# Four rows' statistics moved from VectorE to ScalarE in an SSM kernel's first batch, and a reordered parameter chain behind it

## The chip, the cores and the metric

The kernel runs on one core of one Trainium2 chip. The metric is the device time of one execution in microseconds (us). Before the change it is 687.45 us, the median of three runs (686.68 to 687.59).

## What is computed

The reference is a block with two halves. First a layer normalisation of `u` (2048 tokens x 448 channels), modulated by vectors made from `c`, goes through a long convolution whose kernel is a sum of 256 damped oscillations per channel (S4D). Then a token-mixing MLP follows.

```python
dt = jnp.exp(log_dt)
A = -jnp.exp(log_A_real) + 1j * A_imag
C = (C_real + 1j * C_imag) * dt[:, None]
P = jnp.exp((A * dt[:, None])[:, :, None] * pos[None, None, :])
K = 2.0 * jnp.einsum("dn,dnl->dl", C, P).real
Kf = jnp.fft.rfft(K, L2); Uf = jnp.fft.rfft(u_t, L2)
y = jnp.fft.irfft(Uf * Kf[None, :, :], L2)[:, :, :L]
...
h = _layernorm(x, axis=-1) * (1 + ca) + sa
x = x + ga * _A_ref(h, ...)
h = _layernorm(x, axis=-1) * (1 + cb) + sb
x = x + gb * _B_ref(h, ...)          # W2 gelu(W1 LayerNorm(h))
```

What matters here: the layer normalisation needs mean and variance of all 2048 tokens, and the kernel `K` needs, for each channel and oscillation, a log magnitude (the "exponents") and an angle (the "phases").

## The kernel before

**Stages.** The 448 channels are worked in 28 groups of 16, two steps per group, so 56 steps, in sets of eight (`BATCH`). The whole first part (to about 380 us) makes the convolution kernel step by step and, beside it, normalises and transforms the input; then comes the MLP, which is matmul after matmul. Instructions of TensorE (PE), ScalarE (ACT), VectorE (DVE) and GpSimd (POOL) stand in an order written out by hand; each engine runs its own list in that order and waits where an input isn't there yet.

**A set.** At the first step of each set `window(s)` (L1024) runs first: ScalarE takes logarithms and exponentials there, eight pairs of exponentials into `mag` (L650), with one table of functions. Then follow the eight steps with the table of sines. So ScalarE's table is changed twice a set.

**A step s** is: TensorE's `st_phase(s+1)` (L639, angles into the PSUM tiles `xe` and `xg`, two buffers of each); ScalarE's `st_abs(s)` (L676, L677) and four sines (L686 to L689, two of them in place in `xe` and `xg`); GpSimd's two products `G` (L691, L692) and a magnitude `m` for a later step (L666, L668); VectorE's four products `E` (L693, L694, L698, L699, each 128 x 512), which read `xe` and `xg`; and `st_kgen` (L722), which multiplies `E` and `G` on TensorE. ScalarE copies the result out after every second step (L736), and VectorE adds to it (L741).

**Beside the steps of the first set** (`s` from 0 to 7), in `between()` behind a step's four `E`, VectorE takes the statistics of the input's 16 rows of tiles: `u_stats(r)`, one `bn_stats` and one `bn_aggr` (L537, L538), six rows before step 0 and ten rows by the table `late_rows`, one or two behind each of steps 0 to 5. Row r's mean and variance go to `mv[:, r]`. ScalarE's `logs` in the window of step 8 takes their square roots by logarithm and exponential (L471, L472, tile `rs`), VectorE makes the factor and the shift (`u_scale`, L542 to L546, tile `nm`), GpSimd or ScalarE normalises the rows (L553, L551), and TensorE transforms them (`u_rows`, tile `pu`, L563). VectorE multiplies the result by the modulation into `yt` (L566).

**The parameter chain.** The first 128 channels' parameters are made at the start; those of the second, third and fourth 128 (`chain(q)`, q = 1, 2, 3) are made a few small VectorE instructions at a time: `more(n)` runs the next n pieces of the generator, up to a point ("logs") where it waits for ScalarE's logarithms in the next window. The table `WPACE` says how many pieces each of a window's eight stages e runs, `pace` how many each step runs. Behind the window's logarithms the chain made first the exponents' part (L426, L428 and splits into two halves, L393, L395), then the phases' part (L433 to L443), then the start angle (L447 to L459).

**Deferred work.** `act` and `dve` are lists of deferred instructions that `flush` puts out. What is put on `act` in `between()` stands on ScalarE's list behind that step's sines, and ahead of the next step's.

Of the kernel before, what the change touches and what calls it, by code (L numbers as in the profile page):

```python
# [11 lines left out]
F32 = mybir.dt.float32  # L12
F32R = mybir.dt.float32r
BF16 = mybir.dt.bfloat16
AF = mybir.ActivationFunctionType
ALU = mybir.AluOpType
# [5 lines left out]
L, D, N, F = 2048, 448, 256, 1792  # L22
P = 128
# [10 lines left out]
MAGIC = 1.5 * 2.0**23  # L34
# [187 lines left out]
def tile_adaln_s4d_mixer(ctx, tc, i, out):  # L222
# [21 lines left out]
    with ExitStack() as es:  # L244
        V, S, G, T = nc.vector, nc.scalar, nc.gpsimd, nc.tensor
        tt, ts, stt = V.tensor_tensor, V.tensor_scalar, V.scalar_tensor_tensor
# [19 lines left out]
        xp = spec.enter_context(tc.tile_pool(name="xp", bufs=1))  # L266
# [33 lines left out]
        xt = xp.tile([P, 16, D], F32, name="xt")  # L300
# [37 lines left out]
        for q in range(4):  # L338
            r = slice(32 * q, 32 * q + 1)
# [31 lines left out]
        dt4 = qp.tile([P, 4], F32, name="dt4")  # L371
# [4 lines left out]
        dve, act, late_act = [], [], []  # L376
# [5 lines left out]
        def chain(q):  # L382


            w = N if q < 3 else P
            cr, ci, a, aim = (raws[q][nm][:, 0:w] for nm in ("A_C_real", "A_C_imag", "A_log_A_real", "A_A_imag"))
            xa, ya, s, t, u, ph, p64 = (
                qp.tile([P, N], F32, tag=nm, name=nm)[:, 0:w] for nm in ("xa", "ya", "s", "t", "u", "ph", "p64")
            )

            def split(src, to):
                hl = qp.tile([P, 2, N], F32R, tag="hl", name="hl", bufs=3)[:, :, 0:w]
                V.tensor_copy(hl[:, 0], src)  # L393
                yield
                tt(hl[:, 1], src, hl[:, 0].bitcast(F32), ALU.subtract)  # L395
                for k, v in to:
                    if q < 3:
                        nc.sync.dma_start(pars[q][v, k], hl.bitcast(F32))
                        continue
                    for h in range(2):  # L400
                        r = slice(64 * h, 64 * h + 64)
                        nc.sync.dma_start(pars[q][v, k, 0:64, :, P * h : P * h + P], hl[r].bitcast(F32))
                yield


            S.activation(xa, cr, AF.Abs, scale=0.5)
            S.activation(ya, ci, AF.Abs, scale=0.5)
            stt(s, xa, 2.0**-120, ya, ALU.max, ALU.add)
            yield
            tt(ya, ya, xa, ALU.subtract)  # L410
            yield
            V.reciprocal(xa, s)
            yield
            tt(ya, ya, xa, ALU.mult)
            yield

            ts(t, s, 2.0**-40, 2.0**80, ALU.is_lt, ALU.mult)
            yield
            stt(s, t, 1.0, s, ALU.max, ALU.mult)
            yield  # L420
            tmp[q] = a, s, u, xa, ya
            while q in tmp:
                yield "logs"
            ya = u
            yield from split(a, [(0, 1), (1, 1)])
            stt(s, t, -80 * math.log(2.0) / 2.0**80, s, ALU.mult, ALU.add)  # L426
            yield
            tt(s, ya, s, ALU.add)  # L428
            yield
            yield from split(s, [(2, 1)])  # L430
            yield "exponents"

            ts(ph, aim, dt4[:, q : q + 1], None, ALU.mult)  # L433
            yield
            ts(u, ph, MAGIC, MAGIC, ALU.add, ALU.subtract)
            yield
            tt(ph, ph, u, ALU.subtract)
            yield
            yield from split(ph, [(0, 0)])

            ts(u, ph, MAGIC / 128, MAGIC / 128, ALU.add, ALU.subtract)
            yield
            tt(p64, ph, u, ALU.subtract)  # L443
            yield
            yield from split(p64, [(1, 0)])

            ts(u, cr, 0.0, 0.5, ALU.is_ge, ALU.subtract)  # L447
            yield
            tt(xa, xa, u, ALU.mult)
            yield  # L450
            ts(u, ci, 0.0, 0.5, ALU.is_ge, ALU.subtract)
            yield
            stt(xa, xa, 0.5, u, ALU.add, ALU.mult)
            yield
            stt(xa, ph, 63.0, xa, ALU.mult, ALU.add)
            yield
            ts(u, xa, MAGIC, MAGIC, ALU.add, ALU.subtract)
            yield
            tt(xa, xa, u, ALU.subtract)  # L459
            yield  # L460
            yield from split(xa, [(2, 0)])
# [69 lines left out]
        mv = xp.tile([P, 16, 2], F32, name="mv")  # L531
        rs = xp.tile([P, 16], F32, name="rs")
        nm = xp.tile([P, 16], F32, name="nm")

        def u_stats(r):
            st = xp.tile([P, 6], F32, tag="st", name="st", bufs=2)
            V.bn_stats(st, xt[:, r])  # L537
            V.bn_aggr(mv[:, r], st)  # L538

        def u_scale():  # L540

            tt(nm, rs, rs, ALU.mult)  # L542
            stt(nm, mv[:, :, 1], EPS, nm, ALU.add, ALU.mult)
            ts(nm, nm, -0.5, 1.5, ALU.mult, ALU.add)
            tt(rs, rs, nm, ALU.mult)
            stt(nm, mv[:, :, 0], -1.0, rs, ALU.mult, ALU.mult)  # L546
# [433 lines left out]
        def more(n):  # L980

            for _ in range(n):
                if next(rest, None) in ("logs", "end"):
                    return
# [29 lines left out]
        def window(s):  # L1014
            angle()
            logs(s == 8)
            if s == 8:
                u_scale()
                u_norm(0)
                u_norm(1)  # L1020

            if s == 0:
                st_exponents(s)
            for e in range(BATCH):  # L1024
                st_exp(s + e)

                if e + 1 < BATCH:
                    st_exponents(s + e + 1)
                else:
                    st_phase(s)  # L1030
                mellow()
                if s == 8 and e == 0:
                    tt(mod[1], mod[1], mod[2], ALU.mult)
                flush(dve)
                flush(act)
                flush(late_act)
                if s < 32:
                    more(WPACE[s // 8][e])
                if s == 0 and e >= 4:
                    u_stats(e - 4)  # L1040
                if s == 32 and e == 3:
                    st_kgen(31)
                elif s and e < (2 if s < 32 else 1):
                    st_kgen(s - (2 if s <= 32 else 1) + e)
                elif e == (7 if s == 32 else 5):
                    if s == 8:
                        yks[0] = y0.tile([P, 32, DC], F32, tag="yk", name="yk0")
                    st_s1(s > 16)

                if s in (8, 16):  # L1050
                    some(u_rows, rows, (1, 1, 1, 1, 1, 0, 0, 1)[e])
                elif s == 24 and e != 5:
                    some(u_cols, cols, 1)

                if s == 32 and e == 2:
                    nc.sync.dma_start(t0, i["T0"].rearrange("p (j m) -> p j m", j=2))
                if s == 32 and e == 5:
                    pc_load(1)
                if s >= 40 and e == 2:
                    piece(False)  # L1060
                if s >= 32 and e == 4:
                    piece(pieces[0] < NP, V)
                if s == 0 and e in (4, 5):
                    st_mag2(e - 4)
                    x_load(4 * e - 12, 4, G)
                elif s == 0 and e == 6:
                    x_load(12, 4, G)
                elif s and (e < 2 or s >= 32):
                    st_mag2(s + e)
                if s == 8 and e == 0:  # L1070
                    u_norm(e + 2)
                if s == 0 and e == 3:
                    for r in range(4):
                        dsk_copy(r)
            if s == 0:
                for r in (4, 5):
                    u_stats(r)

                S.activation(one, one, AF.Sin)

        WPACE = [[0] * 8, [0, 2, 3, 4, 5, 5, 5, 5], [0, 5, 4, 4, 4, 4, 4, 4], [2] * 8]
        pace = [0] + [2] * 31
        mod_steps = {3: (1, 0), 4: (1, 1), 5: (2, 0), 6: (2, 1), 12: (0, 0), 13: (0, 1)}
        late_rows = {0: (6, 7), 1: (8,), 2: (9, 10), 3: (11,), 4: (12, 13), 5: (14, 15)}
        tail = NHALF + 3
        for s in range(tail):
            if s == 32:
# [26 lines left out]
            def between():  # L1116
                flush(dve)
                if s == 15:
                    tt(mod[0], mod[0], mod[2], ALU.mult)
                for r in late_rows.get(s, ()):  # L1120
                    u_stats(r)
                if s < len(pace):
                    more(pace[s])

# [244 lines left out]
    with ExitStack() as es:  # L1369
        es.enter_context(tc.manual_schedule(engines={ENG.PE, ENG.Activation, ENG.DVE, ENG.Pool}))  # L1370
        V, S, G = nc.vector, nc.scalar, nc.gpsimd
# [118 lines left out]
```

## Time and profile before

| | |
|---|---|
| median of 3 runs | 687.45 us |
| the profiled execution | 683.26 us |
| its span, first to last instruction | 681.0 us |
| VectorE busy over the span | 447.0 us (66%) |
| ScalarE busy over the span | 438.7 us (64%) |
| GpSimd busy over the span | 271.0 us (40%) |
| TensorE busy over the span | 616.1 us (90%) |

Read such a profile by stages: the shares are averages over a first part in which four engines take turns and a second part, from about 400 us, in which TensorE alone sets the pace. A row of the timeline gives start, duration (us), engine, line, operation, tiles, and in brackets how long the engine sat idle before it and what ended that. A duration is longer than the distance to the next start, since successive instructions of an engine overlap by about 0.1 us; where a sum is made, distances between starts are used.

### The profile page before, as it was taken

To read this page: it belongs to the slowest core of one execution; us is meant where nothing else is said; L and a number is where in the kernel's file an instruction comes from. 1 tells how busy PE (TensorE), PEld (TensorE's weight loads), DVE (VectorE), ACT (ScalarE), POOL (GpSimd) and SP (SyncE) were. 2 spreads that over 40 slices of the span, in tenths; PEclk is the share of its full clock that TensorE was granted. 3 is DMA by queue.
4 is the path that set the end of the run, shared out by engine and by line. 5 is a ranking of instruction groups with operands and counts; after the bars stand their busy time and mean duration, and the time that the engine had idled before them with its cause. 6 is when DMAs were issued, how large, how long until landed. Compare 5 with 4: busy or idle time off the path is not lost. (4 is left out here: it accounts for less than half of the span.)

```text
span 681.0 us, 18308 instructions
## 1 busy us (share of the span) xinstructions
PE 616.1 (90%) x7180; PEld 455.6 (67%) x7180; DVE 447.0 (66%) x880; ACT 438.7 (64%) x880; POOL 271.0 (40%) x329
## 2 busy tenths in 40 slices
PE   1688889879988799999999899999999999999997
PEld 0344445435445466565667667779999999999996
DVE  7598898988589595786966587777422454333331
ACT  6869699879879899999945588877322422222220
POOL 6886378178178787898847100000000000000000
PEclk9989869979989998999999999999999999999999
DMA  4953646659876576354359799956664356555540
GB/s 108 256 179 103 234 157 199 217 188 290 250 240 197 165 164 184 110 155 119 98 140 323 226 265 251 240 133 190 181 198 136 95 149 165 163 165 171 165 119 28
DMA packets 106719, 121.15 MB, mean 178 GB/s; under 512 B 13254, under 2 KB 95178, under 8 KB 106634
## 3 DMA queue, kind: packets, MB, share of 16 engines
q1 hardware_dynamic: 105306, 115.39, 58.9%
q0 software_dynamic: 1328, 4.59, 2.5%
q8 instruction: 57, 0.93, 0.6%
q14 instruction: 28, 0.23, 0.1%
HBM read 84.40 MB, written 34.87 MB: 175 GB/s over the span
## 5 line engine op out<-in xcount | busy, mean ns | idle before, releaser
L207 ACT CAST whi<-w 128x896 fp32r<-128x896 f32 x64 | 59.8, 939 | 133.5 <-PE o L1457 81.0
L691 POOL TENSOR_TENSOR G<-mag,gs 128x512 f32<-128x512 f32 x56 | 72.2, 1290 | 62.6 <-ACT gs L687 60.3
L216 DVE TENSOR_TENSOR wlo<-w,whi 128x896 fp32r<-128x896 f32 x64 | 68.0, 1086 | 40.3 <-ACT whi L207 31.0
L1387 PE MATMUL acc<-h3h,whi 128*128 128x448 f32 x224 | 82.8, 369 | 1.1 <-ACT h3h L1292 1.1
L1388 PE MATMUL acc<-h3l,whi 128*128 128x448 f32 x224 | 81.5, 364 | 1.1 <-DVE h3l L1299 0.9
L1457 PE MATMUL o<-ul,whi 128*128 128x448 f32 x224 | 81.3, 363 | 0.0
L1456 PE MATMUL o<-uh,whi 128*128 128x448 f32 x224 | 81.2, 362 | 0.0
L1389 PE MATMUL acc<-h3h,wlo 128*128 128x448 f32 x224 | 80.7, 360 | 0.0
L1458 PE MATMUL o<-uh,wlo 128*128 128x448 f32 x224 | 80.6, 360 | 0.0
L722 PEld LDWEIGHTS kg<-E,G 128*32 128x32 f32 x3584 | 57.4, 116 | 33.4 <-issue 16.7
L639 PE MATMUL xg<-tab,lph 64*128 64x512 f32 x112 | 63.6, 570 | 11.7 <-DVE E L699 5.0
L639 PE MATMUL xe<-tab,lph 64*128 64x512 f32 x112 | 63.7, 570 | 11.2 <-DVE E L694 6.0
L692 POOL TENSOR_TENSOR G<-mag,gs 128x512 f32<-128x512 f32 x56 | 71.9, 1285 | 0.0
L722 PE MATMUL kg<-E,G 128*32 128x64 f32 x3584 | 67.4, 230 | 4.6 <-issue 3.1
L1460 DVE SCALAR_TENSOR_TENSOR y<-o,b,mod 128x448 f32<-128x448 f32 x16 | 10.9, 684 | 80.3 <-PE o L1458 80.3
L668 POOL TENSOR_TENSOR m<-mag,w 128x512 f32<-128x512 f32 x56 | 59.1, 1055 | 4.4
L1387 PEld LDWEIGHTS acc<-h3h,whi 128*128 128x128 f32 x224 | 42.0, 188 | 14.0 <-ACT h L1297 4.9
L693 DVE TENSOR_TENSOR E<-m,xe 128x512 f32<-128x512 f32 x56 | 38.2, 682 | 15.8 <-ACT xe L686 8.3
L676 ACT ACTIVATE ab<-xe 128x512 f32<-128x512 f32 x56 | 33.9, 605 | 21.7 <-PE xe L639 16.6
L1388 PEld LDWEIGHTS acc<-h3l,whi 128*128 128x128 f32 x224 | 42.1, 188 | 3.8 <-DVE h3l L1299 1.2
L1456 PEld LDWEIGHTS o<-uh,whi 128*128 128x128 f32 x224 | 42.0, 188 | 3.4
L1389 PEld LDWEIGHTS acc<-h3h,wlo 128*128 128x128 f32 x224 | 41.9, 187 | 3.0
(242 smaller groups left out, 1436.5 us busy)
## 6 DMA issues: line engine op xcount, KB each, us to landing
w<-in_B_w_dram SPq DMA_DIRECT2D x64, 224.0 KB
w<-in_B_w_dram SPq DMA_DIRECT2D x32, 448.0 KB
yu_d<-yt SPq DMA_DIRECT2D x16, 448.0 KB
yi<-yu_d SPq DMA_DIRECT2D x16, 448.0 KB
us_d<-uo SPq DMA_DIRECT2D x16, 448.0 KB
u<-us_d SPq DMA_DIRECT2D x32, 224.0 KB
v_d<-vt SPq DMA_DIRECT2D x32, 224.0 KB
vt<-v_d SPq DMA_DIRECT2D x14, 448.0 KB
```

The costliest lines, as they stand in the source:

```text
L207: self.nc.scalar.copy(hi, w)
L216: eng.tensor_tensor(lo, w, hi.bitcast(F32), ALU.subtract)
L639: T.matmul(out[k], lhs[r], rhs[r], start=start, stop=stop)
L691: G.tensor_tensor(Gt[:, 1], mg_, v32(sg), ALU.mult)
L692: G.tensor_tensor(Gt[:, 0], mg_, v32(cg_), ALU.mult)
L722: T.matmul(kgs[g][32 * q : 32 * q + 32, m], Gt[:, c, d], E[:, c, d], start=h == 0 and c == 0 and m == 0, stop=h == 1 and c == 1, skip_grou ...
L1387: nc.tensor.matmul(acc[f], hi[:, fs], h3h[:, r], start=r == 0, stop=False)
L1388: nc.tensor.matmul(acc[f], hi[:, fs], h3l[:, r], start=False, stop=False)
L1389: nc.tensor.matmul(acc[f], lo[:, fs], h3h[:, r], start=False, stop=r == 15)
L1456: nc.tensor.matmul(o, hi[:, ks], uh[kh][:, k], start=kh == 0 and k == 0, stop=False)
L1457: nc.tensor.matmul(o, hi[:, ks], ul[kh][:, k], start=False, stop=False)
L1458: nc.tensor.matmul(o, lo[:, ks], uh[kh][:, k], start=False, stop=kh == 1 and k == 6)
```

## The change

Two edits.

**First batch.** Of the ten rows whose statistics VectorE took behind steps 0 to 5, four (7, 10, 13 and 15) get theirs by two ScalarE passes. `u_mean(r)`, behind the sines of steps 1 to 4, copies the row scaled by 1/D and accumulates: the mean. `u_var(r)`, one step later, has VectorE make the shift -mean/sqrt(D) in one column of `nm`, and ScalarE square the shifted, scaled row and accumulate: the variance.

**The set of step 8.** For q = 1 the phases' seven first instructions (with their splits) are a function `phases()` that runs ahead of the exponents' part. Two of its pieces are run in the window before `u_scale`, and seven more in stage e = 0. The whole chain of q = 1 ends a stage earlier, so that five pieces of q = 2 come into stage e = 7.

```diff
+            if q == 1:
+                yield from phases()
             ya = u
             yield from split(a, [(0, 1), (1, 1)])
...
-            ts(ph, aim, dt4[:, q : q + 1], None, ALU.mult)
...
-            yield from split(p64, [(1, 0)])
+            if q > 1:
+                yield from phases()
...
+        def u_mean(r):
+            junk = xp.tile([P, 2, D], F32, tag="yt", name="junk", bufs=3)[:, 0]
+            S.activation(junk, xt[:, r], AF.Copy, scale=1.0 / D, accum_out=mv[:, r, 0:1])
+
+        def u_var(r):
+
+            junk = xp.tile([P, 2, D], F32, tag="yt", name="junk", bufs=3)[:, 0]
+            ts(nm[:, r : r + 1], mv[:, r, 0:1], -(D**-0.5), None, ALU.mult)
+            act.append(
+                lambda: S.activation(
+                    junk, xt[:, r], AF.Square, scale=D**-0.5, bias=nm[:, r : r + 1], accum_out=mv[:, r, 1:2]
+                )
+            )
...
             if s == 8:
+                more(2)
                 u_scale()
...
-        WPACE = [[0] * 8, [0, 2, 3, 4, 5, 5, 5, 5], [0, 5, 4, 4, 4, 4, 4, 4], [2] * 8]
+        WPACE = [[0] * 8, [7, 2, 1, 2, 3, 5, 5, 5], [0, 5, 4, 4, 4, 4, 4, 4], [2] * 8]
...
-        late_rows = {0: (6, 7), 1: (8,), 2: (9, 10), 3: (11,), 4: (12, 13), 5: (14, 15)}
+        late_rows = {0: (6,), 1: (8,), 2: (9,), 3: (11,), 4: (12,), 5: (14,)}
+        late_means = {1: 7, 2: 10, 3: 13, 4: 15}
...
                 for r in late_rows.get(s, ()):
                     u_stats(r)
+                if s - 1 in late_means:
+                    u_var(late_means[s - 1])
+                if s in late_means:
+                    act.append(partial(u_mean, late_means[s]))
```

**ScalarE's order at steps 2 and 3.** Before, the last two sines of step 2 are followed by step 3's.

```order
L688 ACTIVATE gs<-gs 128x512
L689 ACTIVATE xg<-ab 128x512
L676 ACTIVATE ab<-xe 128x512
L677 ACTIVATE gs<-xg 128x512
L686 ACTIVATE xe<-xe 128x512
```

After, two passes over `xt` stand between them: the square of row 7, which reads `nm`, and the mean of row 10.

```order
L708 ACTIVATE gs<-gs 128x512
L709 ACTIVATE xg<-ab 128x512
L555 ACTIVATE junk,mv<-xt,nm 128x448
L548 ACTIVATE junk,mv<-xt 128x448
L696 ACTIVATE ab<-xe 128x512
L697 ACTIVATE gs<-xg 128x512
L706 ACTIVATE xe<-xe 128x512
```

So step 3's three first ScalarE instructions moved behind two passes, the first of which waits for VectorE's `nm`.

**VectorE's order at step 2.** Before: the four `E` (the last two shown), the statistics of rows 9 and 10, two pieces of the chain, and step 3's first `E`.

```order
L698 TENSOR_TENSOR E<-mag,xg 128x16x32
L699 TENSOR_TENSOR E<-m_425,xg 128x16x32
L537 BN_STATS st<-xt 128x6
L538 BN_AGGR mv<-st 128x2
L537 BN_STATS st<-xt 128x6
L538 BN_AGGR mv<-st 128x2
L412 RECIPROCAL xa<-s 128x256
L414 TENSOR_TENSOR ya<-ya,xa 128x256
L344 MEMSET wm_79 112x1
L693 TENSOR_TENSOR E<-m_472,xe 128x16x32
```

After: one row's statistics, then the shift of row 7.

```order
L718 TENSOR_TENSOR E<-mag,xg 128x16x32
L719 TENSOR_TENSOR E<-m_422,xg 128x16x32
L543 BN_STATS st<-xt 128x6
L544 BN_AGGR mv<-st 128x2
L553 TENSOR_SCALAR nm<-mv 128x1
L427 RECIPROCAL xa<-s 128x256
L429 TENSOR_TENSOR ya<-ya,xa 128x256
L344 MEMSET wm_79 112x1
L713 TENSOR_TENSOR E<-m_471,xe 128x16x32
```

The second row's two instructions became one on a single column; it stands behind all four `E` of its step.

**VectorE's order at the window of step 8.** Before: `u_scale`'s last instruction, the modulation's product, the kernel's addition, and the first `yt`.

```order
L546 SCALAR_TENSOR_TENSOR nm<-mv,rs 128x16
L1033 TENSOR_TENSOR mod_105<-mod_105,mod_106 128x448
L741 TENSOR_TENSOR ks<-ks,dsk 128x4
L566 TENSOR_TENSOR yt<-pu,mod_105 128x448 x2
```

After, seven pieces of the phases stand ahead of the first `yt` (two more stand ahead of `u_scale`).

```order
L566 SCALAR_TENSOR_TENSOR nm<-mv,rs 128x16
L1054 TENSOR_TENSOR mod_105<-mod_105,mod_106 128x448
L761 TENSOR_TENSOR ks<-ks,dsk 128x4
L412 TENSOR_TENSOR ph<-ph,p_462 128x256
L393 CAST hl<-ph 128x256
L395 TENSOR_TENSOR hl<-ph,hl 128x256
L415 TENSOR_SCALAR p_462<-ph 128x256
L417 TENSOR_TENSOR p_462<-ph,p_462 128x256
L393 CAST hl<-p_462 128x256
L395 TENSOR_TENSOR hl<-p_462,hl 128x256
L586 TENSOR_TENSOR yt<-pu,mod_105 128x448 x2
```

The seven moved from behind the third to fifth `yt` to ahead of the first. TensorE's and GpSimd's lists keep their order.

More of the change, by code (lines that the diff above doesn't have):

```diff
@@ L403, in split, with phases @@
                 yield
+            def phases():
+                ts(ph, aim, dt4[:, q : q + 1], None, ALU.mult)
+                yield
+                ts(p64, ph, MAGIC, MAGIC, ALU.add, ALU.subtract)
+                yield
+                tt(ph, ph, p64, ALU.subtract)
+                yield
+                yield from split(ph, [(0, 0)])
+                ts(p64, ph, MAGIC / 128, MAGIC / 128, ALU.add, ALU.subtract)
+                yield
+                tt(p64, ph, p64, ALU.subtract)
+                yield
+                yield from split(p64, [(1, 0)])
             S.activation(xa, cr, AF.Abs, scale=0.5)
@@ L431, in chain @@
             yield "exponents"
-            ts(ph, aim, dt4[:, q : q + 1], None, ALU.mult)
[L434 to L444, printed above, removed]
-            yield from split(p64, [(1, 0)])
+            if q > 1:
+                yield from phases()
             ts(u, cr, 0.0, 0.5, ALU.is_ge, ALU.subtract)
```

## The prediction

> **What bounds the kernel now.** I read the page first: busy shares in 40 slices, then the chain of waits, then a table of stages, and in the stage that the change touches the timeline engine by engine.
>
> The first fence has two rows of the page's slices (17 us each), a row of the table of stages (30 to 60 us: busy PE, PEld, DVE, ACT, POOL, then granted clock, DMA share, GB/s), and the first piece of the chain of waits.
>
> ```profile
> DVE  7598898988589595786966587777422454333331
> ACT  6869699879879899999945588877322422222220
> 30.00:60.00 30.00, 24.44 (x384) 13.79 (x384) 29.50 (x60) 20.21 (x41) 25.49 (x27) 0.94 0.59 182
> 381.84 3.61 DMA v_d<-vt
> ```
>
> The chain goes back only to 382 us, so what bounds the first set must come from its own stage. There VectorE is busy 29.50 of 30 us, ScalarE 20.21: VectorE bounds it on average. Whether ScalarE is really free to take work is a question of order, which the busy share doesn't answer. Step 5 on VectorE:
>
> ```profile
> 54.93 0.69 DVE L693 TENSOR_TENSOR E<-m,xe 128x512 f32<-128x512 f32 x1
> 57.33 0.62 DVE L537 BATCH_NORM_STATS2 st<-xt 128x6 f32<-128x448 f32 x1
> 58.08 0.59 DVE L537 BATCH_NORM_STATS2 st<-xt 128x6 f32<-128x448 f32 x1
> 58.82 0.69 DVE L693 TENSOR_TENSOR E<-m,xe 128x512 f32<-128x512 f32 x1
> ```
>
> Four `E` take 2.40 us, one row's statistics 0.75, and the step 3.89. On ScalarE (steps 6 and 7, the end of the window's logarithms, and VectorE's first use of them):
>
> ```profile
> 54.39 0.60 ACT L676 ACTIVATE ab<-xe 128x512 f32<-128x512 f32 x1 [0.52 <-PE xe L639]
> 55.37 0.60 ACT L686 ACTIVATE xe<-xe 128x512 f32<-128x512 f32 x1
> 58.52 0.60 ACT L676 ACTIVATE ab<-xe 128x512 f32<-128x512 f32 x1 [1.03 <-PE xe L639]
> 65.21 0.22 ACT L472 ACTIVATE rs<-rs 128x16 f32<-128x16 f32 x1
> 65.46 0.18 DVE L542 TENSOR_TENSOR nm<-rs 128x16 f32<-128x16 f32 x1 [1.07 <-ACT rs L472]
> 65.67 0.17 DVE L543 SCALAR_TENSOR_TENSOR nm<-mv,nm 128x16 f32<-128x16 f32 x1
> ```
>
> ScalarE starts step 6's angles at 54.39, before VectorE starts step 5's `E` (54.93). It runs a step ahead, so VectorE never waits for a sine. That lead is what the change touches.
>
> **Part 1: four rows' statistics.** VectorE loses four rows, 4 x 0.75 = 3.0 us, and gains four single columns at 0.21 (65.46 to 65.67): 2.2 us less, if that were all.
>
> ScalarE gains eight passes over 448 columns. A square with accumulation is in the MLP's normalisation, and a plain cast of that size in a group's row (fields: total us, mean ns, idle):
>
> ```profile
> 386.09 0.67 ACT L1243 ACTIVATE sq<-xt,mean 128x448 f32<-128x448 f32 x1 [1.10 <-issue]
> 386.67 0.19 ACT L1243 ACTIVATION_READ_ACCUMULATOR sq<-xt,mean 128x1 f32 x1
> 386.89 0.29 ACT L1244 ACTIVATE rs<-ss,small_t 128x1 f32<-128x1 f32 x1
> L1298 ACT CAST h3h<-h 128x448 fp32r<-128x448 f32 x15 | 8.5, 567 | 0.5
> ```
>
> The square costs 0.80 (386.09 to 386.89). No mean by ScalarE is in the trace; by the cast it is 0.57 + 0.19 less an overlap of 0.1 = 0.66, by the square 0.80. I take 0.70.
>
> The new wait is dearer than the passes. By the order, row 7's square stands on ScalarE behind step 2's sines and ahead of step 3's, and it reads a shift that VectorE makes behind step 2's four `E` and a row's statistics. Queued behind it on ScalarE: row 10's mean and step 3's angles, for which VectorE's `E` of step 3 waits. The same holds at steps 3, 4 and 5 (the last without a mean). So the lead of a step is gone, and a step goes round one loop: four `E` 2.40, one row 0.75, shift 0.21, square 0.80, mean 0.70, ScalarE's `ab`, `gs` and sine of `xe` 1.58 (54.39 to the end of the row of 55.37), two hand-overs of about 0.05: 6.54 us. At step 5, without a mean, 5.84.
>
> Where it starts:
>
> ```profile
> 34.71 0.68 DVE L693 TENSOR_TENSOR E<-m,xe 128x512 f32<-128x512 f32 x1
> 37.85 1.31 DVE L408 SCALAR_TENSOR_TENSOR s<-xa,ya 128x256 f32<-128x256 f32 x1
> 39.20 1.38 DVE L410 TENSOR_TENSOR ya<-ya,xa 128x256 f32<-128x256 f32 x1
> 40.51 0.68 DVE L693 TENSOR_TENSOR E<-m,xe 128x512 f32<-128x512 f32 x1
> 37.60 1.28 POOL L691 TENSOR_TENSOR G<-mag,gs 128x512 f32<-128x512 f32 x1
> 38.85 1.45 POOL L692 TENSOR_TENSOR G<-mag,gs 128x512 f32<-128x512 f32 x1
> 90.29 0.42 DVE L410 TENSOR_TENSOR ya<-ya,xa 128x256 f32<-128x256 f32 x1
> ```
>
> Step 1's `E` begin at 34.71 less the removed row, 33.96. Behind them L408 and L410 took 1.31 and 1.38 where L410 elsewhere takes 0.42: each ended 0.3 us after a GpSimd product did (38.85 and 40.30), so they waited for it. A row earlier, L408 is issued at 37.1, ahead of the product of 37.60, and L410 gets the next gap, at 38.85. Step 2's `E` then start at 39.2 (between 38.6 and the old 40.5).
>
> From there: step 3 at 45.7, step 4 at 52.3, step 5 at 59.1 (0.26 more at step 4 for the addition of L741, the first row below: least, middle and longest of three in ns), step 6 at 64.9.
>
> ```profile
> L741 DVE TENSOR_TENSOR ks<-ks,dsk x3: 157/335/780, 53.2 to 66.9; 128x4 f32<-128x4 f32 x3
> 58.82 0.69 DVE L693 TENSOR_TENSOR E<-m,xe 128x512 f32<-128x512 f32 x1
> 101.83 0.60 ACT L676 ACTIVATE ab<-xe 128x512 f32<-128x512 f32 x1
> 104.83 1.41 ACT L551 ACTIVATE xt<-xt,nm,rs 128x448 f32<-128x448 f32 x2
> ```
>
> Before, step 6's `E` started at 58.82, so the loop costs 6.1 there. Step 6's angles start 1.68 ahead of its `E`, at 63.2; six ScalarE instructions of a step take 3.0 (101.83 to 104.83); step 7's start at 66.2 instead of 58.52. From there to `rs` ScalarE worked without a gap (6.9 us). So `rs`, `nm` and with them the whole window of step 8 come **7.7 us later**. VectorE sat idle 1.07 us for `rs` already, so nothing covers it.
>
> A term on top: the shift itself is a small VectorE instruction while GpSimd works. L741, on four columns, took 0.16 to 0.78 us there. If the shift waits for a GpSimd instruction it costs 0 to 1.2 us at each of steps 3 to 5, so 0 to 3.6; I take 0.5, since it falls near the gap between GpSimd's products and the next magnitude.
>
> The Trainium skill ("SBUF — State Buffer", Who interferes with whom) says that a VectorE instruction with two SBUF inputs, or in a two-port mode, and a GpSimd instruction block each other for a whole instruction. The rows of 37.85 and 39.20 agree; by that page a column's shift in a two-port mode would wait as well, and the term would lie nearer 2 us.
>
> **Part 2: the phases ahead of the exponents.** Nine instructions leave the window's busy part.
>
> ```profile
> 78.29 0.41 DVE L437 TENSOR_TENSOR ph<-ph,u 128x256 f32<-128x256 f32 x1
> 80.08 1.15 DVE L566 TENSOR_TENSOR yt<-pu,mod 128x448 f32<-128x448 f32 x2
> 66.58 3.11 POOL L553 TENSOR_SCALAR xt<-xt,rs,nm 128x448 f32<-128x448 f32 x4 [3.37 <-DVE nm L546]
> 69.55 1.15 DVE L566 TENSOR_TENSOR yt<-pu,mod 128x448 f32<-128x448 f32 x2 [2.46 <-PE pu L563]
> 70.62 0.56 DVE L393 CAST hl<-A_log_A_real 128x256 fp32r<-128x256 f32 x1
> 71.21 0.82 DVE L395 TENSOR_TENSOR hl<-A_log_A_real,hl 128x256 fp32r<-128x256 f32 x1
> ```
>
> Five of them took 1.79 (78.29 to 80.08), 0.36 each, so nine take 3.2. Two go into the idle time ahead of `nm` (1.07), hidden. Seven go into the 2.46 us ahead of the first `yt`, where they would fit at 0.36; but GpSimd normalises rows just then (3.11 for four), and the two small instructions beside its work took 0.56 and 0.82. At 0.7 each the seven take 4.9, put the first `yt` off by 2.4, and leave 0.8 of the 3.2. Bounds: 2.9 gained if nothing collides, 0.5 lost if each takes 0.8 and GpSimd's rows are put off too. I take 0.5 gained.
>
> Five pieces of the third 128 channels' chain come into stage 7 of the window, out of steps 8 to 10.
>
> ```profile
> 86.98 0.69 DVE L693 TENSOR_TENSOR E<-m,xe 128x512 f32<-128x512 f32 x1 [0.55 <-ACT xe L686]
> 90.64 0.68 DVE L693 TENSOR_TENSOR E<-m,xe 128x512 f32<-128x512 f32 x1
> 91.91 1.10 ACT L767 COPY yk<-y 128x512 f32<-128x512 f32 x2
> 93.24 1.75 DVE L412 RECIPROCAL xa<-s 128x256 f32<-128x256 f32 x1
> 96.70 0.67 DVE L693 TENSOR_TENSOR E<-m,xe 128x512 f32<-128x512 f32 x1
> ```
>
> They are a reciprocal (1.75) and four of some 0.42: 3.4 us more ahead of step 8's `E` (0.55 of it in VectorE's idle time), 3.4 less behind. Behind, step 9 to step 10 took 6.06 of which the reciprocal and a product were 2.2; ScalarE's own pace there is 3.0 for the sines and 1.1 for two copies, so most is given back. I take 0.2 gained, between 2.5 gained and 1.5 lost (ScalarE needn't follow). The stores that the splits issue on SP's queue move ahead with them; what reads them comes with step 16's group and isn't hurried or delayed by it, so they cost nothing; were the queue held up by them, the `yt` stores behind would be late by a store's issue, 0.5 to 1 us, still well ahead of their reader.
>
> **The sum.** 7.7 + 0.5 - 0.5 - 0.2 = 7.5 us slower. The profiled execution (683.26: the span of 681.0 and 2.26 around it) becomes 690.8, its span 688.5. The median of the runs lies 4.2 above the profiled time; I carry the difference over: 687.45 + 7.5 = **695.0**.
>
> **The rivals.**
>
> *VectorE stays the bound* (0.05). For it: 29.50 of 30 us busy, and ScalarE has 10 us of idle time per 30. Then the first set gains the 2.2 us, and part 2 up to 2.9: 682.4 to 685.3, **faster**, 684 in the middle. The Trainium skill ("Perfetto Trace Analysis", Optimizing Scalar/DVE Operations) gives that rule: with a saturated VectorE, moving some work to ScalarE may make sense. Against it is the order alone: the square waits for VectorE's shift, and step 3's sines stand behind the square. It decides if step 3's sines start before step 2's four `E` end, which the order excludes; what is left is that I misjudge how long the loop is. The signs meet where each of the four loops is 1.9 us (7.5 / 4) shorter, at 4.7.
>
> *The set of step 8 pays it back* (0.14). The first set costs its 7.7, but the seven pieces do fit (2.9) and steps 8 to 10 give their 2.5: +2.3, **689.8**. For it: VectorE is the only engine without gaps there. Against it: GpSimd's normalisation in the very gap.
>
> *The shift waits for GpSimd at each of three steps* (0.13): 3.6 instead of 0.5, and the seven pieces lose: +11, **698.5**. For it: L741's 0.78. Against it: a product of two tiles isn't a single column.
>
> *No change within the noise* (0.04): loop shorter than I think and payback both, about 687.5. The change not doing what it says is no case of its own: the order shows the four rows gone from VectorE.
>
> **How the numbers follow.** Forecast 0.64. A difference of 0.2% (1.4 us) is about what a measurement of this kernel can tell from no change. The forecast's own bounds: 7.7 less 0.6 for an earlier step 2 and less 4.0 of the 5.4 that part 2 can give at most, with the shifts free, is 690.5; 7.7 with 2.6 for the shifts and 1.0 lost in part 2 is 698.8. The range of 690.0 to 699.0 holds the forecast, the third rival and a good part of the second; left out are the first, no change and the rest of the second, under 0.2. Faster 0.05, same 0.04, slower 0.91 (0.64 + 0.14 + 0.13).
>
> **What would show it.** Right: VectorE's row for 30 to 60 us falls well under 29.50 and its `E` of steps 3 to 6 wait for ScalarE's `xe`, with starts 6.5 us apart; ScalarE's waits get a line for the square's pass on VectorE's shift, some 1 to 2 us at each of four steps; `rs` ends at about 73 and the first `yt` at 78 to 80. Wrong: `E` starts under 5 us apart, or ScalarE without a wait ahead of the squares; then VectorE bounds, and the first rival holds. If `rs` is 8 late but step 10's `E` start under 3 us late, the second holds. If the shift's rows show over 0.5 us, the third.

## The result, and the profile after

The changed kernel is slower: its median is 689.35 us over 20 runs (686.17 to 695.25). The kernel before, run beside it, has a median of 685.53 us over 20 runs (680.77 to 689.06). The ratio is 1.006, with an interval of 1.0036 to 1.0083, so some 4.1 us; a ratio here is estimated from the single runs and can differ from the quotient of the medians by up to 0.002. Left out of the ratios, as slow runs, are three of the 31 of before in the experiments (689.92 to 721.27 us) and one of the shift ahead (964.03). The prediction of 695.0 had the right sign, but it was too high by 5.65, and the time lies below its range. Of that, 1.9 us is the base: 687.45 was the median of three runs, and 20 runs give 685.53. The rest is the change itself, forecast at 7.5 and measured at 3.8 (689.35 less 685.53; 4.1 by the ratio).

The profiled execution took 687.83 us, with a span of 685.6 (before: 683.26 and 681.0). These are the same two rows of the page's slices (VectorE, ScalarE) as before:

```profile
DVE  7586899888679595795977587777422454443331
ACT  6867799889879998999945578877322332222220
```

And the row of the table of stages for 30 to 60 us (busy PE, PEld, DVE, ACT, POOL, then granted clock, DMA share, GB/s):

```profile
30.00:60.00 30.00, 20.51 (x308) 10.87 (x308) 24.03 (x49) 19.66 (x46) 20.01 (x22) 0.78 0.60 186
```

VectorE is busy 24.03 us there instead of 29.50: it no longer bounds this stage. ScalarE, which was given eight more passes, is busy no longer than before (19.66 against 20.21), since the steps come more slowly and some of its sines fall behind the 60 us. So nobody is full; the engines wait for each other. VectorE's timeline of the changed kernel shows where (first `E` of steps 3 to 6; for step 4 also the third `E`, the addition behind the four and the shift; and the first use of `rs`):

```profile
44.82 0.69 DVE L713 TENSOR_TENSOR E<-m,xe 128x512 f32<-128x512 f32 x1 [0.77 <-issue]
...
51.26 0.69 DVE L713 TENSOR_TENSOR E<-m,xe 128x512 f32<-128x512 f32 x1 [1.47 <-issue]
...
52.72 0.69 DVE L718 TENSOR_TENSOR E<-mag,xg 128x512 f32<-128x512 f32 x1 [0.17 <-ACT xg L709]
...
53.92 0.37 DVE L761 TENSOR_TENSOR ks<-ks,dsk 128x4 f32<-128x4 f32 x1
...
54.95 0.12 DVE L553 TENSOR_SCALAR nm<-mv 128x1 f32<-128x1 f32 x1
57.97 0.69 DVE L713 TENSOR_TENSOR E<-m,xe 128x512 f32<-128x512 f32 x1 [2.90 <-issue]
...
63.85 0.69 DVE L713 TENSOR_TENSOR E<-m,xe 128x512 f32<-128x512 f32 x1 [2.34 <-issue]
...
72.25 0.17 DVE L562 TENSOR_TENSOR nm<-rs 128x16 f32<-128x16 f32 x1 [1.78 <-ACT rs L478]
```

ScalarE's timeline over the gap ahead of 57.97:

```profile
55.11 0.67 ACT L555 ACTIVATE junk<-xt,nm 128x448 f32<-128x448 f32 x1 [2.42 <-DVE nm L553]
...
55.78 0.56 ACT L548 ACTIVATE junk<-xt 128x448 f32<-128x448 f32 x1
...
56.34 0.57 ACT L696 ACTIVATE ab<-xe 128x512 f32<-128x512 f32 x1
...
57.29 0.59 ACT L706 ACTIVATE xe<-xe 128x512 f32<-128x512 f32 x1
```

Read the two together: VectorE makes the shift at 54.95; ScalarE, which had stood idle 2.42 us for it, squares, takes the next mean, and only then comes to step 5's angles; its sine of `xe` ends at 57.88, and VectorE, idle for 2.90 us, starts step 5's `E` at 57.97. The trace puts that idle time down to "issue", though the sine that this `E` reads ended 0.09 us before it. In the table of waits for 30 to 70 us, ScalarE's line gives the sum of the four waits (total us, times, longest):

```profile
ACT junk L555 <- DVE nm L553: 10.0, 4, 4.3
```

Behind the window of step 8, VectorE's timeline shows a reciprocal of the third 128 channels and the first `E` of steps 8, 9 and 10:

```profile
91.30 1.75 DVE L427 RECIPROCAL xa<-s 128x256 f32<-128x256 f32 x1
94.70 0.68 DVE L713 TENSOR_TENSOR E<-m,xe 128x512 f32<-128x512 f32 x1
97.83 0.68 DVE L713 TENSOR_TENSOR E<-m,xe 128x512 f32<-128x512 f32 x1
101.30 0.67 DVE L713 TENSOR_TENSOR E<-m,xe 128x512 f32<-128x512 f32 x1
```

The reciprocal now stands ahead of step 8. Before, it stood between steps 9 and 10, which were 6.06 us apart; now they are 3.47 apart.

### The profile page after: what moved, and what is told of

The parts are those of the page before. It is cut to its first block, busy times and chain, and to the rows that moved or that the text cites. A ratio compares the mean times of both kernels' runs of the same rounds, so it can differ in the third digit from the quotient of the medians.

```text
span 685.6 us, 18318 instructions
## 1 busy us (share of the span) xinstructions
PE 616.1 (90%) x7180; PEld 456.6 (67%) x7180; DVE 444.9 (65%) x876; ACT 443.3 (65%) x896; POOL 271.0 (40%) x329
## 5 line engine op out<-in xcount | busy, mean ns | idle before, releaser
L1484 PEld LDWEIGHTS o<-uh,wlo 128*128 128x128 f32 x224 | 42.1, 188 | 3.3
L1483 PEld LDWEIGHTS o<-ul,whi 128*128 128x128 f32 x224 | 41.9, 187 | 3.0
```

The lines of the kernel that those rows point to most:

```text
L1483: nc.tensor.matmul(o, hi[:, ks], ul[kh][:, k], start=False, stop=False)
L1484: nc.tensor.matmul(o, lo[:, ks], uh[kh][:, k], start=False, stop=kh == 1 and k == 6)
```

## The experiments

**The theories.** Mine: a loop through the shift costs the first set some 7 us (the prediction had 7.7), and part 2 gives some of it back by hiding its pieces and by moving five pieces of the third 128 channels ahead of step 8. The rivals: that the passes' own work costs ScalarE the time, not the wait; and on part 2, that either the five moved pieces or the hidden nine do the whole of the payback.

The same marks are read in every run: the start of the first `E` of a step (L693 before, its counterpart in the others), less the start of step 0's `E` in the same run, which lies ahead of the change (30.25 to 31.77 us). The table gives how much later that is than in the profiled execution of before (us; minus is earlier), and the measured ratio.

| kernel | step 3 | step 6 | step 8 | step 10 | step 15 | step 52 | ratio (interval) |
|---|---|---|---|---|---|---|---|
| after | -1.07 | +5.62 | +8.31 | +5.19 | +4.19 | +5.08 | 1.006 (1.0036 to 1.0083) |
| part 1 alone | -1.07 | +5.61 | +7.54 | +7.53 | +7.34 | +8.19 | 1.0108 (1.0069 to 1.0147) |
| part 2 alone | -0.02 | -0.01 | +1.21 | -1.80 | -2.91 | -1.68 | 0.9982 (0.995 to 1.0014) |
| shift ahead | -0.90 | -1.70 | +1.02 | -1.99 | -2.80 | -4.38 | 0.9947 (0.9925 to 0.9969) |
| narrow passes | -1.80 | +3.08 | +5.79 | +2.78 | +4.20 | +3.01 | 1.004 (1.0015 to 1.0065) |
| without the five | -1.04 | +5.66 | +5.88 | +5.87 | +5.10 | +4.47 | 1.0079 (1.0057 to 1.0101) |
| two pieces in the gap | -1.03 | +5.67 | +10.80 | +7.79 | +6.85 | +6.49 | 1.0085 (1.0061 to 1.0109) |
| shift ahead, without the five | -0.88 | -0.77 | +0.15 | +0.14 | +0.61 | +0.71 | 0.9981 (0.9959 to 1.0004) |

Each row is one trace; the last experiment shows how far two traces of the same instructions can lie apart. The first four experiments were measured against 31 runs of before (median 684.84), the last three against 17 (685.03). Diffs are against the changed kernel.

**Part 1 alone.** The statistics move, the chain stays in its old order and at its old pace.

```diff
-            if q == 1:
-                yield from phases()
...
-            if q > 1:
-                yield from phases()
+            yield from phases()
...
-                more(2)
                 u_scale()
...
-        WPACE = [[0] * 8, [7, 2, 1, 2, 3, 5, 5, 5], [0, 5, 4, 4, 4, 4, 4, 4], [2] * 8]
+        WPACE = [[0] * 8, [0, 2, 3, 4, 5, 5, 5, 5], [0, 5, 4, 4, 4, 4, 4, 4], [2] * 8]
```

> Part 1 alone: the four rows by ScalarE, the chain's order and paces as before. Theory (a loop of VectorE and ScalarE of 6.4 us a step costs 7 us in the first set; part 2 gave 3 to 4 of it back): the first set as in the changed kernel, rs about 6.8 us late, and nothing given back behind it, so 7 us slower at the end, a ratio of 1.010. Rival (part 1 costs what the whole change costs, about 4, and part 2 gives nothing): the window or steps 8 to 10 give 3 us back here too, ratio 1.006.

Median 691.13 us over 8 runs, ratio 1.0108 (1.0069 to 1.0147): 7.4 us. VectorE's timeline:

```profile
72.81 0.17 DVE L559 TENSOR_TENSOR nm<-rs 128x16 f32<-128x16 f32 x1 [2.53 <-ACT rs L475]
...
94.51 0.69 DVE L710 TENSOR_TENSOR E<-m,xe 128x512 f32<-128x512 f32 x1 [0.55 <-ACT xe L703]
...
100.77 1.75 DVE L427 RECIPROCAL xa<-s 128x256 f32<-128x256 f32 x1
...
104.22 0.67 DVE L710 TENSOR_TENSOR E<-m,xe 128x512 f32<-128x512 f32 x1
```

`nm` comes at 72.81 where before had 65.46, 7.35 us late, and from there on everything keeps its old distances: step 8 is 7.54 late, step 10 7.53 and step 15 7.34; step 52 is 8.19 late in this trace, and the end 7.4 by the ratio. So the first set's term stands, nothing behind it repairs the delay by itself, and what the changed kernel wins back after step 8 is part 2's doing.

**Part 2 alone.** The statistics stay on VectorE.

```diff
-        late_rows = {0: (6,), 1: (8,), 2: (9,), 3: (11,), 4: (12,), 5: (14,)}
-        late_means = {1: 7, 2: 10, 3: 13, 4: 15}
+        late_rows = {0: (6, 7), 1: (8,), 2: (9, 10), 3: (11,), 4: (12, 13), 5: (14, 15)}
+        late_means = {}
```

> Part 2 alone: all ten rows by VectorE as before, the phases ahead of the exponents. Theory: the nine moved pieces lie in idle time, so step 10's products start 2.5 to 3.5 us earlier than before and stay so: ratio 0.995 to 0.9965. Rival (part 2 is worth nothing, what was given back in steps 8 to 10 was slack that any late start finds): step 10 within 0.5 us of before, ratio 1.000.

Median 682.79 us over 12 runs, ratio 0.9982 (0.995 to 1.0014): 1.2 us, and the interval includes no change. That is less than the theory said, and so is step 10, 1.80 early where 2.5 to 3.5 were expected. In its trace, step 8 is 1.21 late and step 15 is 2.91 early. The same turn stands between steps 8 and 15 of the changed kernel (+8.31 to +4.19). Taken on top of part 1 it is worth 3.3 us by the ratios (from 1.0108 to 1.006), in the traces 3.15 at step 15 (7.34 less 4.19) and 3.11 at step 52. Whether it is worth more there than alone isn't shown: at step 15 the two are 2.91 and 3.15, and the intervals of 1.0108 and 1.006 overlap.

**The shift ahead.** The same instructions on the same engines, but VectorE makes the shift ahead of a step's four `E`, not behind them.

```diff
+        def u_shift(r):
+            ts(nm[:, r : r + 1], mv[:, r, 0:1], -(D**-0.5), None, ALU.mult)
...
-            ts(nm[:, r : r + 1], mv[:, r, 0:1], -(D**-0.5), None, ALU.mult)
...
+                if s - 1 in late_means:
+                    u_shift(late_means[s - 1])
                 st_step(s, between)
```

> The whole change, but VectorE makes each row's shift ahead of its step's four products instead of behind them; the same instructions otherwise. Theory (the wait of the square for the shift is what costs): no loop; steps 2 to 5 are paced by ScalarE's 4.2 to 4.7 us, step 6's products start 0 to 2 us earlier than before, and with part 2 the end is 3 to 5 us earlier: ratio 0.993 to 0.996. Rival (ScalarE's eight passes, 5 us of work, are what costs): steps stay at 6 us or more, the ratio 1.003 to 1.006.

Median 681.59 us over 12 runs, ratio 0.9947 (0.9925 to 0.9969): faster than before and than the changed kernel. VectorE's timeline:

```profile
49.01 0.15 DVE L551 TENSOR_SCALAR nm<-mv 128x1 f32<-128x1 f32 x1
...
49.08 0.68 DVE L715 TENSOR_TENSOR E<-m,xe 128x512 f32<-128x512 f32 x1
...
52.41 0.69 DVE L715 TENSOR_TENSOR E<-m,xe 128x512 f32<-128x512 f32 x1
...
56.77 0.69 DVE L715 TENSOR_TENSOR E<-m,xe 128x512 f32<-128x512 f32 x1 [0.86 <-POOL m L690]
...
65.17 0.17 DVE L564 TENSOR_TENSOR nm<-rs 128x16 f32<-128x16 f32 x1 [1.79 <-ACT rs L478]
```

ScalarE's line of the waits, 30 to 70 us:

```profile
ACT junk L557 <- DVE nm L551: 2.9, 2, 1.7
```

ScalarE's wait for the shift falls from 10.0 us to 2.9, the `E` of steps 4 to 6 start 3.33 and 4.36 apart instead of 6.71 and 5.88, and `nm` comes at 65.17. Against its own step 0 that is 0.06 later than before; with the shift behind the `E` it was 7.4 later. So part 1's price hangs on the place of one instruction of 0.12 us: with that instruction ahead of the `E`, the eight passes cost next to nothing by `nm`. That rules out the rival as it was put, that their work costs whatever the order. (The last experiment has the same first set, and there `nm` comes 1.70 later than before; its trace gives another reason for that.)

The rows also show what part 1 can gain once the order is right. VectorE is 1.70 early at step 6, but `nm` is not early, and its idle time for `rs` grows from 1.07 to 1.79. ScalarE's timeline (step 7's angles and the end of the logarithms) tells why:

```profile
58.24 0.60 ACT L698 ACTIVATE ab<-xe 128x512 f32<-128x512 f32 x1
...
64.92 0.21 ACT L478 ACTIVATE rs<-rs 128x16 f32<-128x16 f32 x1
```

ScalarE works without a gap from 45.34, where its last wait for a shift ends, to the end of `rs`; the stretch from 58.24 is 6.9 us, the same 6.9 as before from 58.52. It reaches step 7 hardly sooner, since it carries the passes. What this kernel gains over before comes after that, by steps 8 to 15, and at step 15 it stands where part 2 alone stands (-2.80 and -2.91). At step 52 the two traces lie apart (-4.38 and -1.68), and why was not tried. The Trainium skill ("Perfetto Trace Analysis", Optimizing Scalar/DVE Operations) says that with a saturated VectorE it may pay to move work to ScalarE. In this set it did not: 7.4 us late in the one order and level at `nm` in the other.

**Narrow passes.** The eight passes run over 8 columns instead of 448, with the wait in its place; the kernel leaves 440 columns out of the four rows' statistics.

```diff
-            S.activation(junk, xt[:, r], AF.Copy, scale=1.0 / D, accum_out=mv[:, r, 0:1])
+            S.activation(junk[:, 0:8], xt[:, r, 0:8], AF.Copy, scale=1.0 / D, accum_out=mv[:, r, 0:1])
...
-                    junk, xt[:, r], AF.Square, scale=D**-0.5, bias=nm[:, r : r + 1], accum_out=mv[:, r, 1:2]
+                    junk[:, 0:8], xt[:, r, 0:8], AF.Square, scale=D**-0.5, bias=nm[:, r : r + 1], accum_out=mv[:, r, 1:2]
```

> The whole change with each of the eight passes over 8 of the row's 448 columns, so that 440 columns are left out of the four rows' statistics; the wait stands. Theory (the loop): a pass takes about 0.3 us instead of 0.66 and 0.56, the loop 5.8 instead of 6.4, step 6's products start 2.5 to 3 us late instead of 5, the end 1.5 to 2.5 late: ratio 1.002 to 1.004. Rival (the passes' work costs): nearly all of it goes and the removed rows show, 3 to 5 us faster than before: ratio 0.993 to 0.996.

Median 686.65 us over 12 runs, ratio 1.004 (1.0015 to 1.0065). VectorE's timeline, first `E` of steps 4, 5 and 6:

```profile
50.43 0.69 DVE L713 TENSOR_TENSOR E<-m,xe 128x512 f32<-128x512 f32 x1 [0.74 <-issue]
...
56.44 0.69 DVE L713 TENSOR_TENSOR E<-m,xe 128x512 f32<-128x512 f32 x1 [2.16 <-issue]
...
61.95 0.69 DVE L713 TENSOR_TENSOR E<-m,xe 128x512 f32<-128x512 f32 x1 [1.97 <-issue]
```

With hardly any work left in the passes the loop still takes 6.01 and 5.51 us a step (6.71 and 5.88 with it), and step 6 is still 3.08 late. The passes lengthen the loop, by 2.5 of the 5.62 us at step 6 (5.62 less 3.08), but they don't make it.

**Without the five.** Stage 7 of the window of step 8 runs no piece of the third 128 channels.

```diff
-        WPACE = [[0] * 8, [7, 2, 1, 2, 3, 5, 5, 5], [0, 5, 4, 4, 4, 4, 4, 4], [2] * 8]
+        WPACE = [[0] * 8, [7, 2, 1, 2, 3, 5, 5, 0], [0, 5, 4, 4, 4, 4, 4, 4], [2] * 8]
```

> The whole change without the five pieces of the third channels' chain in stage 7 of the window of step 8; they go back to steps 8 to 10. Theory (what part 2 gives is the nine hidden pieces; the five only decide whether it shows ahead of step 8 or behind it): against the changed kernel step 8's products start 3 to 4 us earlier, step 11's and the end are within 0.7 us of it: step 8 at +4, the end at +4.5 against before, ratio 1.004 to 1.008. Rival (the gain is the five pieces' leaving steps 8 to 10 for a window with room for them): step 8 hardly earlier (under 1 us), the end 2 to 3 us later than the changed kernel: +7, ratio 1.010.

Median 689.69 us over 6 runs, ratio 1.0079 (1.0057 to 1.0101). VectorE's timeline:

```profile
93.54 0.69 DVE L713 TENSOR_TENSOR E<-m,xe 128x512 f32<-128x512 f32 x1 [1.54 <-ACT xe L706]
...
99.80 1.75 DVE L427 RECIPROCAL xa<-s 128x256 f32<-128x256 f32 x1
...
103.25 0.67 DVE L713 TENSOR_TENSOR E<-m,xe 128x512 f32<-128x512 f32 x1
```

The reciprocal is back between steps 9 and 10, which are 6.06 apart again. The expected gain ahead of step 8 came out smaller, 2.43 us (+8.31 to +5.88), because VectorE then waits 1.54 for ScalarE's sine. So the five cost 2.4 ahead of step 8 and give 3.3 back by step 15 (4.12, the fall from +8.31 to +4.19, less the 0.78 from +5.88 to +5.10): 0.9 net at step 15. At step 52 that is gone: there the trace without the five is 0.61 earlier (+4.47 against +5.08), while the ratios put it 1.3 later, with intervals that overlap. So at the end neither the theory nor its rival is decided.

**Two pieces in the gap.** Only the two pieces ahead of `u_scale` stay ahead of the first `yt`; the seven beside GpSimd's normalisation go behind it.

```diff
-        WPACE = [[0] * 8, [7, 2, 1, 2, 3, 5, 5, 5], [0, 5, 4, 4, 4, 4, 4, 4], [2] * 8]
+        WPACE = [[0] * 8, [0, 2, 3, 5, 5, 5, 5, 5], [0, 5, 4, 4, 4, 4, 4, 4], [2] * 8]
```

> The whole change with only two pieces of the phases ahead of the first product yt; the seven follow it, and the five of the next chain stay in stage 7. Theory (the seven in the gap put the first yt off by 1.4 us but spare 2.5 to 3 behind): the first yt 1.4 us earlier against rs than in the changed kernel, step 8's products 1 to 2 us later, the end 1 to 2 us later: +5.5 to +6.5 against before, ratio 1.008. Rival (the collision with GpSimd costs what the gap saves): step 8 and the end within 0.5 us of the changed kernel, ratio 1.006.

Median 689.65 us over 6 runs, ratio 1.0085 (1.0061 to 1.0109). VectorE's timeline, the end of `u_scale` and the first `yt`:

```profile
73.36 0.17 DVE L566 SCALAR_TENSOR_TENSOR nm<-mv,rs 128x16 f32<-128x16 f32 x1
...
76.61 1.16 DVE L586 TENSOR_TENSOR yt<-pu,mod 128x448 f32<-128x448 f32 x2 [2.47 <-PE pu L583]
```

The same place in the changed kernel, with three of the seven pieces (from the first to the third) between:

```profile
73.08 0.17 DVE L566 SCALAR_TENSOR_TENSOR nm<-mv,rs 128x16 f32<-128x16 f32 x1
...
73.78 0.42 DVE L412 TENSOR_TENSOR ph<-ph,p 128x256 f32<-128x256 f32 x1
74.24 0.53 DVE L393 CAST hl<-ph 128x256 fp32r<-128x256 f32 x1
74.80 0.82 DVE L395 TENSOR_TENSOR hl<-ph,hl 128x256 fp32r<-128x256 f32 x1
...
77.71 1.15 DVE L586 TENSOR_TENSOR yt<-pu,mod 128x448 f32<-128x448 f32 x2
```

The gap of 2.47 us is filled by seven pieces that take 3.93 (73.78 to 77.71), 0.56 each. The first `yt` comes 4.63 behind `nm` instead of 3.25, so it is put off by 1.4. Against that, the seven are worth 2.49 at step 8 (+10.80 to +8.31), 2.66 at step 15 and 1.41 at step 52; the ratios' intervals (1.0061 to 1.0109 here, 1.0036 to 1.0083 for the changed kernel) overlap.

**Shift ahead, without the five.** The shift ahead, as above, and this line, to see the five pieces without the late first set.

```diff
-        WPACE = [[0] * 8, [7, 2, 1, 2, 3, 5, 5, 5], [0, 5, 4, 4, 4, 4, 4, 4], [2] * 8]
+        WPACE = [[0] * 8, [7, 2, 1, 2, 3, 5, 5, 0], [0, 5, 4, 4, 4, 4, 4, 4], [2] * 8]
```

> The shift ahead of its step's products, and the five pieces back in steps 8 to 10: the version to beat the kernel before by most. Theory as for the one without the five pieces: step 8's products 3 us earlier than with the shift ahead alone, the end within 0.7 us of it, 3 to 5 us earlier than before: ratio 0.993 to 0.9965. Rival: the end 2 to 3 us later than the shift ahead alone, ratio 0.998 to 1.000.

Median 683.67 us over 12 runs, ratio 0.9981 (0.9959 to 1.0004). Against the shift ahead with the five (0.9947) it is 2.3 us slower by the ratios, although the two intervals still overlap. So here the rival's numbers came, not the theory's. In the traces step 15 is 3.4 later. But 1.6 of that stands at step 7 already, where the two kernels have run the same instructions: VectorE waited 1.77 us for ScalarE ahead of step 6, and ScalarE for TensorE (rows of ScalarE and of VectorE):

```profile
56.10 0.60 ACT L698 ACTIVATE ab<-xe 128x512 f32<-128x512 f32 x1 [0.64 <-PE xe L661]
57.76 0.69 DVE L715 TENSOR_TENSOR E<-m,xe 128x512 f32<-128x512 f32 x1 [1.77 <-ACT xe L708]
```

TensorE was slow there: from 45 to 55 us its granted clock was 0.68 in this trace and 1.00 in the shift ahead's, and the four matmuls of L504 ahead of step 6's angles took 3.35 us instead of 1.77. So the 1.6 belongs to this execution and not to the pieces. That leaves 1.8 for the five here, and 0.9 in the pair above.

## Where the prediction failed and where it held

The sign and the loop were right. The step that failed is the price of part 2: it was put at 0.7 us gained and gave 3.1 to 3.3. The time lies 0.65 below the range, and the base, 1.9 too high, adds to that: with 685.53 the same range would have begun at 688.1.

**The loop: right, in part by luck.** From step 2 to step 6 the first `E` were forecast 6.5, 6.6, 6.8 and 5.8 apart; they are 6.16, 6.44, 6.71 and 5.88 apart. Step 2 was forecast at 39.2 and came at 38.66, which is 39.25 when the 0.59 by which this run's step 0 was early is added. From step 4 to step 5 the loop's sum can be read off starts in the two timelines: `E` and the addition 2.94, a row 0.75, shift 0.16, square 0.67, mean 0.56, sines 1.54, hand-over 0.09, together 6.71. Two errors cancel in it: the passes were taken 0.27 too long, and the four `E` 0.27 too short, since they took 2.66 (51.26 to 53.92) and not 2.40. In the loop the third `E` waits for ScalarE's last sine (the row of 52.72), a wait that the forecast had left out. Part 1 was forecast at 7.7 and measured at 7.4 (4.7 to 10.1 by the ratio's interval).

**The passes' sizes: a little high.** The square keeps ScalarE 0.67 us (55.11 to 55.78) and the mean 0.56 (55.78 to 56.34), where I took 0.80 and 0.70. The read of the accumulator overlaps with the next pass.

**The shift behind GpSimd: 0, not 0.5.** All four shifts took 0.12 us, three of them inside one of GpSimd's magnitudes; the third rival is out.

**Part 2: here the prediction failed.** The step that said the seven pieces take "4.9, put the first `yt` off by 2.4, and leave 0.8 of the 3.2", and the one that took 0.2 for the five moved pieces, both put the gain too low. Together they gave 0.7 us; the runs show 3.1 to 3.3 (part 1 alone against both parts). The seven took 3.93, not 4.9: I had taken 0.7 for each from two neighbours of 0.56 and 0.82, but only three of the seven took 0.70 to 0.82 (the row of 74.80 is one; the two ahead of it took 0.42 and 0.53). The first `yt` was put off by 1.4, not 2.4. The hidden pieces, all nine, are worth 1.7 at step 8, where a wait of 1.54 for ScalarE (0.55 in part 1 alone) takes some of it, and 2.2 at step 15 (part 1 alone, +7.54 and +7.34, against without the five, +5.88 and +5.10); I took 0.5, inside bounds of 2.9 gained and 0.5 lost. The five are worth 0.9 to 1.8 at step 15; I took 0.2, inside bounds of 2.5 gained and 1.5 lost.

So 8.2 less 0.7 was forecast, and by the ratios 7.4 less 3.3 was found: an error of 0.8 on part 1 with its shift, and of 2.6 on part 2.

**The second rival was half of what happened.** It said that if `rs` is 8 late but step 10's `E` under 3 us late, the set of step 8 pays it back. Step 8 is 8.31 late, step 10 5.19 and step 15 4.19: half is paid back, in the place that the rival named, though the seven pieces did not fit their gap as it had them. The forecast and this rival stood as two cases of 7.5 and 2.3, and the time came out between them. In the sum each unknown of part 2 was taken below the middle of its own bounds: 0.5 where the middle is 1.2, 0.2 where it is 0.5.

**The first rival is out.** VectorE's 24.03 us of 30 show that it stopped being the bound, as the order had said.

**What stays open.** How much of the payback reaches the end is not settled to a microsecond: part 2 is worth 1.2 us by itself (not told from nothing) and 3.3 on top of part 1 (from two ratios whose intervals overlap), and the five pieces' net at step 15 is 0.9 in the one pair and 1.8 in the other, and -0.6 at step 52 of the first. Nor was it tried why the delay of after against before grows from 4.19 to 5.08 between steps 15 and 52.

## What to carry to other kernels

When work moves from a full engine to one with idle time, first look for what the moved work waits for and what stands behind it in the receiving engine's list: a small input that is made behind the long instructions of a step turns two engines that run a step apart into one loop, and here 0.12 us of work in the wrong place, with the passes and sines queued behind it, cost 7.4 us. Make such an input ahead of the long instructions. And price a rearrangement that costs in one stage and gives in the next with a middle value for each stage and with the marks at both ends (here steps 8 and 15), not with the worst price for each piece.

## What was new about the hardware

**A one-column instruction did not wait for GpSimd.** VectorE's timeline of the changed kernel, the shift and the instruction behind it:

```profile
48.24 0.12 DVE L553 TENSOR_SCALAR nm<-mv 128x1 f32<-128x1 f32 x1
48.28 1.04 DVE L432 TENSOR_SCALAR t<-s 128x256 f32<-128x256 f32 x1
```

GpSimd's, at that time:

```profile
48.12 1.05 POOL L688 TENSOR_TENSOR m<-mag,w 128x512 f32<-128x512 f32 x1
```

The shift took 0.12 us inside GpSimd's magnitude, and so did those of 54.95 and 61.39; the same operation over 256 columns, issued at its heels, took 1.04 and ended 0.15 us behind that magnitude (49.32 and 49.17). In the shift ahead, with GpSimd idle, that instruction took 0.26:

```profile
48.36 0.26 DVE L432 TENSOR_SCALAR t<-s 128x256 f32<-128x256 f32 x1
```

The Trainium skill ("SBUF — State Buffer", Who interferes with whom) has a VectorE instruction in a two-port mode shut out for the whole of a GpSimd instruction that was issued before it; the row of 48.28 agrees, and the row of 48.24 shows that this single column was not held up.

**The granted clock isn't the cause of the loop's delay.** From 30 to 60 us it was 0.94 before and 0.78 after, which could be taken for one. With the same first set, part 1 alone had 0.94 there (and its `E` at the same distances):

```profile
30.00:60.00 30.00, 20.64 (x308) 11.06 (x308) 24.03 (x50) 19.10 (x45) 20.02 (x21) 0.94 0.61 184
```

**One kernel's runs spread** by 8.3 us over 20 (680.77 to 689.06), which is how a median of three could be 1.9 off.
